# New cost figures for a list scheduler: engine handoffs, activation table loads and DMAs in a linear-attention plus SwiGLU kernel

## The chip, the cores and the metric

The program runs on one core of a Trainium2 chip. The metric is device time in microseconds (us) per execution; medians are over several executions, and all executions told here are fast, with the granted TensorE clock above 0.99 of full speed. PE is TensorE (the matmul engine), DVE is VectorE, ACT is ScalarE, POOL is GpSimd, SP is the engine whose queue issues the DMAs.

## The reference

Batch 1, 2048 tokens, width 1024, inner width 3584, 32 heads; inputs in bfloat16.

```python
x = A_x
xn = layernorm(x)
q, k, v = heads(xn @ A_wqkv)
pq, pk = phi(q), phi(k)                       # phi(t) = (t + 1 if t > 0 else exp(t)) + 1e-6
kv = einsum("bhsd,bhse->bhde", pk, v)
z  = sum over s of pk
num, den = pq @ kv, (pq . z) + 1e-6
s = (num / den) @ A_wo
g = silu((silu(xn @ B_w_gate) * (xn @ B_w_up)) @ B_w_down)
return x + s * g
```

## The kernel before

The kernel does not write its instructions in the order in which they run. It records some thousand operations in program order, each with what it reads and writes, and with an estimate of its cost. A list scheduler, at build time, plays the recorded program through a simple model of the core and so fixes one static order for each engine. A second pass adds the semaphore waits. At run time each engine works through its own list in that order. **The model's figures thus cost nothing at run time; they decide only which instruction stands before which.**

These are the parts that the change touches:

```python
LAT = {"pe": 0.25, "act": 0.3, "dve": 0.3, "pool": 0.3}      # from an engine's end to its consumer
# ... Plan.schedule(), inner loop: for each engine e that has candidates a, at its free time t
if e == "pe":
    # only the next WINDOW (6) unscheduled PE operations in program order are candidates
    rdy = [o for o in cand if o.ready <= t + 0.05]
    o = min(rdy, key=lambda o: o.idx) if rdy else min(cand, key=lambda o: (o.ready, o.idx))
else:
    rdy = [o for o in a if o.ready <= t]
    o = min(rdy, key=lambda o: (o.dl - o.boost, o.idx)) if rdy else min(a, key=lambda o: (o.ready, o.dl))
s = max(t, o.ready)
# ... the engine whose operation can start first is taken
if o.sem is not None:                      # a DMA
    free[e] = s + 0.08
    b = max(s + 1.0, dma_free)
    dma_free = b + o.nbytes / 230e3
    o.done = dma_free + 1.8
else:
    free[e] = s + o.busy
    o.done = s + o.busy + o.lat
# ...
for q in o.succs:
    q.ready = max(q.ready, o.done)
# ... cost of an activation, of a DMA issue
act: nel(o) / 1200.0 + (0.055 if src == "ps" else 0.095)
dma: 0.08
```

Start-up, in program order (cut). `ln_tile` is the layer norm of 128 tokens, `t_tile` its transposes, `p_piece(tile, 0 for K or 1 for V, half)` eight matmuls in two groups of four; `combos` are DVE sums of weight blocks:

```python
ln_tile(0); t_tile(0); ln_tile(1)
p_piece(0, 0, 1)
p_piece(0, 0, 0)
t_tile(1)
p_piece(1, 0, 1)
# ... loads of tiles 4 and 5, p_piece(1, 0, 0), ln_tile(2), p_piece(0, 1, 1), t_tile(2), combos(KVV[0]) ...
```

Of the kernel before, what the change touches and what calls it, by code (L numbers as in the profile page):

```python
# [9 lines left out]
ACT = mybir.ActivationFunctionType  # L10
# [5 lines left out]
GRAN = 256  # L16


class Op:
    __slots__ = ("eng", "fn", "busy", "lat", "nbytes", "sem", "preds", "succs", "idx", "dl", "start", "done",  # L20
                 "ev", "pecum", "npred", "ready", "urgent", "boost")


class Region:
# [6 lines left out]
class Plan:  # L31
# [1 line left out]


    ENGS = ("pe", "act", "dve", "pool", "sp")
    LAT = {"pe": 0.25, "act": 0.3, "dve": 0.3, "pool": 0.3}

    def __init__(self, window, lead):
        self.ops = []
# [6 lines left out]
    def op(self, eng, reads, writes, fn, busy, sem=None, nbytes=0, urgent=0.0, cow=None, after=None):  # L46


        o = Op()
        o.eng, o.fn, o.busy, o.sem, o.nbytes, o.urgent = eng, fn, busy, sem, nbytes, urgent  # L50
        o.lat = 0.0 if sem is not None else self.LAT[eng]
        o.boost = 0.0
        o.idx = len(self.ops)
        preds = set()
        for r in reads:
            for k in r.keys:
                preds.update(self.lastw.get(k, ()))
        if cow is not None:
            preds.update(cow.preds)
        if after is not None:  # L60
            preds.add(after)
        for r in writes:
            for k in r.keys:
                if cow is None:
                    preds.update(self.lastw.get(k, ()))
                    preds.update(self.readers.get(k, ()))
        for r in reads:
            for k in r.keys:
                self.readers.setdefault(k, []).append(o)
        for r in writes:  # L70
            for k in r.keys:
                if cow is None:
                    self.lastw[k] = [o]
                    self.readers[k] = []
                else:
                    self.lastw[k].append(o)
        o.preds = preds
        o.succs = []
        for p in preds:
            p.succs.append(o)  # L80
        o.pecum = self.pecum
        if eng == "pe":
            self.pecum += busy
            self.lastpe = o
        self.ops.append(o)
        return o

    def schedule(self):
        ops = self.ops
        for o in reversed(ops):  # L90
            d = o.pecum if o.eng == "pe" else o.pecum + 30.0
            for s in o.succs:
                extra = (4.0 + o.nbytes / 200e3) if o.sem is not None else o.busy + o.lat
                d = min(d, s.dl - extra)
            o.dl = d - o.urgent
        pes = [o for o in ops if o.eng == "pe"]
        cum = [o.pecum + o.busy for o in pes]
        for o in ops:
            if o.sem is not None and o.succs:
                k = bisect_right(cum, o.dl - self.lead) - 1  # L100
                if k >= 0 and pes[k] not in o.preds:
                    o.preds.add(pes[k])
                    pes[k].succs.append(o)
        for o in ops:
            o.npred = len(o.preds)
            o.ready = 0.0
        free = {e: 0.0 for e in self.ENGS}
        dma_free = 0.0
        avail = {e: [] for e in self.ENGS}
        pe_next = deque(o for o in ops if o.eng == "pe")  # L110
        for o in ops:
            if o.npred == 0:
                avail[o.eng].append(o)
        order = []
        done = set()
        total = len(ops)
        while len(order) < total:
            best = None
            for e in self.ENGS:
                a = avail[e]  # L120
                if not a:
                    continue
                t = free[e]
                if e == "pe":
                    lim = None
                    n = 0
                    for o in pe_next:
                        if n >= self.window:
                            lim = o.idx
                            break  # L130
                        n += 1
                    cand = [o for o in a if lim is None or o.idx < lim]
                    if not cand:
                        continue
# [3 lines that stand above are left out]
                    rdy = [o for o in a if o.ready <= t]  # L138
                    o = min(rdy, key=lambda o: (o.dl - o.boost, o.idx)) if rdy else min(a, key=lambda o: (o.ready, o.dl))
                s = max(t, o.ready)  # L140
                if best is None or s < best[0]:
                    best = (s, e, o)
            s, e, o = best
            o.start = s
            if o.sem is not None:
                free[e] = s + 0.08
                b = max(s + 1.0, dma_free)
                dma_free = b + o.nbytes / 230e3
                o.done = dma_free + 1.8
            else:  # L150
                free[e] = s + o.busy
                o.done = s + o.busy + o.lat
            avail[e].remove(o)
            if e == "pe":
                done.add(o)
                while pe_next and pe_next[0] in done:
                    pe_next.popleft()
            order.append(o)
            for q in o.succs:
                q.npred -= 1  # L160
                q.ready = max(q.ready, o.done)
                if q.npred == 0:
                    avail[q.eng].append(q)
        self.order = order
        return order
# [55 lines left out]
def build_kernel(nc, A_x, A_wqkv, A_wo, B_w_gate, B_w_up, B_w_down, out, WINDOW=6, NWARM=14, NPE=4, LEAD=12.0):  # L221
# [12 lines left out]
    with ExitStack() as es:  # L234
# [99 lines left out]
        def nel(ap):  # L334
            n = 1
            for s in ap.shape[1:]:
                n *= s
            return n

        def act(reads, writes, o, i, func, src="ps", **kw):  # L340
            return PL.op("act", reads, writes, lambda h: h.activation(o, i, func, **kw),  # L341
                         nel(o) / 1200.0 + (0.055 if src == "ps" else 0.095))

        def dve(reads, writes, fn, n, rate=0.96):
            return PL.op("dve", reads, writes, fn, n / (rate * 1000.0) + 0.07)
# [2 lines left out]
            return dve(reads, writes, lambda h: h.tensor_tensor(o, a, b, op), nel(o), 1.92 if fast else 0.96)  # L348

        def dma(reads, writes, o, i, s, nbytes, cow=None, after=None):  # L350
            return PL.op("sp", reads, writes, lambda h: h.dma_start(o, i), 0.08, sem=s, nbytes=nbytes, cow=cow,
                         after=after)

        class Ring:
# [320 lines left out]
        def t_tile(i):  # L675
            s = xnslot[i]
            xa = s.ap(FP16)
            ar, j, m = xt_dest(i)
            dst = ar.at(j * 8 * KB, 8 * KB, FP16).rearrange("p (k t) -> p k t", t=512)[:, :, m * 128:(m + 1) * 128]
            if i >= NPE:  # L680
                PL.op("sp", [s.r], [xt_r(i)], lambda h: h.dma_start_transpose(dst, xa), 0.08, sem=dsem("tx%d" % (i % 2)),
                      nbytes=400 * KB)
                return
            if not tb:
                tb.extend((balloc_part(), balloc_part()))
            for q, halves in enumerate(((0, 4), (4, 4)) if i == 0 else ((0, 8),)):
                k0, n = halves
                b = tb[(i + q) % 2]
                pb = ps[b][:, 0:n * 64].bitcast(FP16).rearrange("p (k t) -> p k t", t=128)
                pe_tr([s.r, ident_r], [bank_r[b]],  # L690
                      [(pb[:, k, :], xa[:, (k0 + k) * 128:(k0 + k + 1) * 128], ident[:, :]) for k in range(n)])
                xr = xt_r(i, k0, n)
                if q == 0 or i == 0:
                    act([bank_r[b]], [xr], dst[:, k0:k0 + n], pb, ACT.Identity)
                else:
                    dve([bank_r[b]], [xr], lambda h, k0=k0, n=n, pb=pb: h.tensor_copy(dst[:, k0:k0 + n], pb), n * 128)
# [524 lines left out]
        def d_set(p, c, Sx, sv):  # L1221
# [7 lines left out]
            def fin(i, j):  # L1229
# [18 lines left out]
                def turn_dma():  # L1248
                    o = pt_ring.take()
                    oa = o.ap(FP16).rearrange("p (m n) -> p m n", n=128)  # L1250
                    PL.op("sp", [g.r], [o.r], lambda h: h.dma_start_transpose(oa, g.ap(FP16)), 0.08,
                          sem=dsem("tp%d%d" % (link, o.k)), nbytes=200 * KB, urgent=60.0 * last)
                    tt([o.r, q.r], [q.r], xv[:, :, i * 128:i * 128 + 128], oa, xv[:, :, i * 128:i * 128 + 128], ALU.add,
                       True)
                    done()
# [196 lines left out]
```

## Time and profile before

| | before |
|---|---|
| median of the runs made beside the changed kernel | 731.93 us (731.23 to 732.62, 4 runs) |
| profiled execution | 729.5 us |
| PE, DVE, ACT busy | 98%, 84%, 55% |
| table loads on ACT | 10, of 1.28 us each |

From the page of the kernel before: busy time of each engine (share of the span, number of instructions), and the chain that ended last, by engine.

```profile
PE 715.9 (98%) x3942; PEld 371.1 (51%) x3942; DVE 612.8 (84%) x1443; ACT 400.5 (55%) x759; POOL 14.1 (2%) x35
...
PE 85%; ACT 7%; DVE 5%; issue 2%; POOL 0%; ACTq 0%; DVEq 0%; POOLq 0%
```

PE looks full. But a busy share is a poor measure for this engine: the Trainium skill says so (Perfetto Trace Analysis, Identifying the Most-Contended Engine). Two lines of the timeline of PE in the kernel before, in the steady part (start, length of the merged run, engine, line, what, count):

```profile
40.03 1.03 PE L210 MATMUL ps<-H,W 128*128 128x512 f16 x4
40.90 1.03 PE L210 MATMUL ps<-H,X 128*128 128x512 f16 x4
```

The second four matmuls start 0.87 us after the first four, so 0.216 us each; that agrees with the skill's figure of N / 2.4 + 2.5 ns for one isolated matmul of N columns (TensorE: Matmul & The Clock Gate, Back-to-back issue gap), and that page's 131 ns for sustained 512-column matmuls is not what this trace shows. A record of such a matmul lasts 0.379 us in the table of groups, though. Neighbours overlap by 0.163 us, so a wait of up to 0.163 us between two matmuls leaves "busy" unbroken.

I therefore use a second measure throughout, the **excess**: for each pair of neighbouring matmul records, the distance between their starts less (columns / 2.4 + 2.5) ns, summed over a stretch. 48 pairs of small denominator matmuls run side by side and give -5.08 us; they are left out. Where one matmul record is missing, the distance is exactly one pitch too long; that is counted as zero. In the kernel before the excess is 16.22 us of 729.5: 6.48 us in the first 120 us (about 2.7 of them slow warm-up matmuls on zeros). The rest of the run is matmuls at full pitch, 1.43 us before the first one and 5.03 us from the start of the last one to the end. So a new order can gain at most some 13.5 us, or 1.9% (an estimate: the excess less that of the warm-up). Every excess comes from one traced execution of its kernel.

Who PE waited for in the kernel before (total us, times, longest us):

```profile
PE ps L210 <- ACT TM L341: 1.7, 2, 1.3
PE ps L210 <- POOL ident L391: 1.4, 1, 1.4
PE ps L210 <- DVE ps L348: 1.4, 5, 0.4
PE ps L217 <- DVE TM L348: 1.1, 1, 1.1
PE ps L210 <- ACT X L341: 0.8, 2, 0.5
PE ps L210 <- ACT ps L341: 0.8, 3, 0.3
PE ps L217 <- ACT W L341: 0.4, 1, 0.4
PE ps L210 <- ACT H L341: 0.2, 1, 0.2
```

No DMA is in it. PE at start-up (start, length of the merged run, engine, line, what, count; in brackets: idle time just before, and what ended it):

```profile
8.27 1.04 PE L210 MATMUL ps<-H,X 128*128 128x512 bf16 x4 [0.47 <-ACT X L341]
9.15 0.61 PE L217 MATMUL ps<-ident,W 128*128 128x128 f16 x8
9.59 9.96 PE L210 MATMUL ps<-H,X 128*128 128x512 bf16 x44
...
20.25 4.49 PE L210 MATMUL ps<-H,X 128*128 128x512 bf16 x20 [0.24 <-ACT H L341]
25.19 0.62 PE L217 MATMUL ps<-ident,W 128*128 128x128 f16 x8 [0.45 <-ACT W L341]
...
27.70 1.04 PE L210 MATMUL ps<-H,X 128*128 128x512 bf16 x4 [0.38 <-ACT X L341]
...
31.78 1.90 PE L210 MATMUL ps<-H,W 128*128 128x512 f16 x8 [0.25 <-DVE ps L348]
```

DVE at start-up, 23.7 to 28.0 us. The first line, `nmean`, is the last step of DVE for the layer norm of a tile. Further on, five halves of layer-norm statistics of later tiles (24.91 to 27.41; three are cut) stand before the sums `W<-X` at 28.02. PE uses these from 28.57 on.

```profile
23.70 0.16 DVE L666 SCALAR_TENSOR_TENSOR nmean<-mv,rstd 128x1 f32<-128x1 f32 x1 [0.44 <-POOL rstd L658]
...
24.91 0.69 DVE L649 BATCH_NORM_STATS2 stats<-W 128x6 f32<-128x512 bf16 x1
...
27.41 0.68 DVE L649 BATCH_NORM_STATS2 stats<-W 128x6 f32<-128x512 bf16 x1
28.02 0.41 DVE L348 TENSOR_TENSOR W<-X 128x512 f16<-128x512 f16 x1
```

And a table load on ACT with what surrounds it. PE issues one matmul at 136.66 and then nothing until 138.31, waiting for the activation that had to wait for the load:

```profile
136.37 1.28 ACT L341 ACT_TABLE_LOAD   x1
...
136.66 0.38 PE L210 MATMUL ps<-H 128*128 128x512 bf16 x1
...
137.66 0.60 ACT L341 ACTIVATE TM<-ps 128x512 f16<-128x512 f32 x1
...
138.31 0.88 PE L210 MATMUL ps<-H 128*128 128x512 bf16 x3 [1.27 <-ACT TM L341]
```

The previous activation ends at 136.35 and the next starts at 137.66, so a switch of tables costs 1.3 us here between the records, nearly all of it the load. By the distance of starts, which is 1.93 us across the switch and 0.48 us between the two activations before it, it costs some 1.45 us.

### The profile page before, as it was taken

Reading aid. Unit: us, or ns where it says so; the run is one execution under the profiler, and the core shown is the slowest. Engines: PE = TensorE matmul, PEld = TensorE weight load, DVE = VectorE, ACT = ScalarE, POOL = GpSimd, SP = SyncE. Lnnn points to the kernel's source line nnn. Section 1 sums busy time; section 2 is a strip of 40 time slices with the busy share of each in tenths; the row PEclk is TensorE's granted clock in tenths of the full one; section 3 lists DMA queues with packets and bytes.
Section 4 is the critical chain, followed back from the end, with each engine's and each line's share of the span. In section 5 each row is a group of like instructions: output and inputs, shape, how many; then the busy total and the mean of one; then the engine's idle time right before and its main releaser. Section 6 shows DMA issues by size and latency. Waiting matters only on the chain.

```text
span 729.5 us, 10728 instructions
## 1 busy us (share of the span) xinstructions
PE 715.9 (98%) x3942; PEld 371.1 (51%) x3942; DVE 612.8 (84%) x1443; ACT 400.5 (55%) x759; POOL 14.1 (2%) x35
## 2 busy tenths in 40 slices
PE   8999999999999999999999999999999999999996
PEld 3444444455555555554444445555555555544442
DVE  6999868979989998898555989999999888865662
ACT  3776654787659665654111177676966756511111
POOL 2111000000000000000000000000000000000000
PEclk9999999999999999999999999999999999999999
DMA  8443235135255343324279554134515343546633
GB/s 291 113 104 85 44 107 181 59 107 168 73 159 139 129 143 129 94 73 132 79 186 245 145 165 149 62 116 120 172 59 188 102 130 118 143 123 181 164 89 87
DMA packets 135668, 94.02 MB, mean 129 GB/s; under 512 B 32960, under 2 KB 131520, under 8 KB 135616
## 3 DMA queue, kind: packets, MB, share of 16 engines
q1 hardware_dynamic: 135616, 93.34, 44.9%
q8 instruction: 31, 0.51, 0.3%
q14 instruction: 21, 0.17, 0.1%
HBM read 75.50 MB, written 10.62 MB: 118 GB/s over the span
## 4 chain that ended last, share of the span: by engine, by line
PE 85%; ACT 7%; DVE 5%; issue 2%; POOL 0%; ACTq 0%; DVEq 0%; POOLq 0%
PE ps L210 85%; ACT H L341 3%; ACT TM L341 2%; DVE W L348 2%; DVE H L348 1%; DVE TM L348 1%; ACT ps L341 1%; DVE ps L348 1%; ACT L341 1%; DVE stats L649 0%; DVE stats L653 0%; DVE TM L724 0%; PE ps L217 0%; DVE X L348 0%; POOL rstd L658 0%
## 5 line engine op out<-in xcount | busy, mean ns | idle before, releaser
L210 PE MATMUL ps<-X,W 128*128 128x512 f16 (+1 forms) x1232 | 268.0, 358 | 1.1 <-ACT ps L341 0.5
L341 ACT ACTIVATE TM<-ps 128x512 f16<-128x512 f32 (+2 forms) x345 | 184.2, 553 | 147.8 <-PE ps L210 143.9
L210 PE MATMUL ps<-H,W 128*128 128x512 f16 (+2 forms) x1168 | 256.4, 369 | 0.5 <-DVE ps L348 0.5
L348 DVE TENSOR_TENSOR W<-W 128x256 f16<-128x256 f16 (+5 forms) x440 | 176.4, 437 | 7.2 <-DMA W<-in_B_w_down_dram 7.0
L210 PEld LDWEIGHTS ps<-H,W 128*128 128x128 f16 (+1 forms) x1168 | 113.5, 98 | 124.1 <-DVE ps L348 2.3
L210 PEld LDWEIGHTS ps<-X,W 128*128 128x128 f16 (+1 forms) x1232 | 119.3, 98 | 102.8 <-ACT ps L341 2.2
L348 DVE TENSOR_TENSOR ps<-ps,TM 128x256 f32<-128x256 f32 (+1 forms) x234 | 123.5, 531 | 15.0 <-PE ps L210 14.0
L341 ACT ACTIVATE ps<-ps 128x512 f32<-128x512 f32 (+1 forms) x164 | 81.9, 499 | 72.2 <-PE ps L210 70.1
L210 PE MATMUL ps<-P,W 128*128 128x512 f16 (+1 forms) x496 | 104.7, 329 | 0.7 <-ACT TM L341 0.4
L341 ACT ACTIVATE H<-ps 128x512 f16<-128x512 f32 (+1 forms) x126 | 75.0, 602 | 54.5 <-PE ps L210 54.2
L210 PEld LDWEIGHTS ps<-P,W 128*128 128x128 f16 (+1 forms) x496 | 48.3, 98 | 37.9 <-ACT ps L341 1.0
L348 DVE TENSOR_TENSOR H<-H 128x1024 f16<-128x1024 f16 (+4 forms) x106 | 66.1, 640 | 1.0 <-ACT H L341 0.5
L348 DVE TENSOR_TENSOR TM<-ps,TM 128x512 f32<-128x512 f32 (+1 forms) x60 | 40.7, 678 | 24.0 <-PE ps L210 23.7
L210 PE MATMUL ps<-W 128*128 128x256 f16 (+1 forms) x278 | 56.5, 289 | 0.6 <-DVE ps L348 0.4
L348 DVE TENSOR_TENSOR H<-H,TM 128x512 f16<-128x512 f16 x112 | 44.8, 415 | 14.0 <-ACT H L341 13.8
L341 ACT ACTIVATE TM<-TM 128x512 f16<-128x512 f32 (+1 forms) x61 | 37.9, 624 | 33.4 <-DVE TM L348 32.5
L210 PEld LDWEIGHTS ps<-W 128*128 128x128 f16 (+1 forms) x278 | 26.1, 98 | 21.3 <-DVE ps L348 2.3
L210 PE MATMUL ps<-H,X 128*128 128x512 bf16 (+1 forms) x136 | 32.2, 379 | 1.2 <-ACT X L341 0.8
L210 PE MATMUL ps<-TM,W 128*128 128x256 f16 (+1 forms) x138 | 27.8, 283 | 0.3 <-DVE ps L348 0.3
L348 DVE TENSOR_TENSOR P<-H 128x1024 f16<-128x1024 f16 x28 | 19.0, 686 | 9.2 <-PE ps L210 9.2
L723 DVE TENSOR_SCALAR TM<-TM 128x512 f16<-128x512 f16 x64 | 17.7, 285 | 10.5 <-ACT TM L341 10.3
L348 DVE TENSOR_TENSOR H<-ps,TM 128x512 f16<-128x512 f32 (+1 forms) x35 | 23.9, 682 | 2.3 <-PE ps L210 1.7
(81 smaller groups left out, 394.9 us busy)
## 6 DMA issues: line engine op xcount, KB each, us to landing
W<-in_B_w_down_dram SPq DMA_DIRECT2D x16, 896.0 KB, 5.8
W<-in_B_w_gate_dram SPq DMA_DIRECT2D x12, 1024.0 KB, 5.4
W<-in_B_w_up_dram SPq DMA_DIRECT2D x12, 1024.0 KB, 5.5
W<-in_A_x_dram SPq DMA_DIRECT2D x16, 256.0 KB, 3.0
H<-in_A_wqkv_dram SPq DMA_DIRECT2D x8, 512.0 KB, 8.2
H<-r_scratch SPq DMA_DIRECT2D x32, 128.0 KB, 3.4
W<-m_scratch SPq DMA_DIRECT2D x4, 1024.0 KB, 5.9
s_scratch<-TM SPq DMA_DIRECT2D x32, 128.0 KB, 2.8
```

Source lines behind the costliest of these rows:

```text
L210: last = h.matmul(o, l, r, start=st, stop=sp, skip_group_check=True)
L341: return PL.op("act", reads, writes, lambda h: h.activation(o, i, func, **kw), nel(o) / 1200.0 + (0.055 if src == "ps" else 0.095))
L348: return dve(reads, writes, lambda h: h.tensor_tensor(o, a, b, op), nel(o), 1.92 if fast else 0.96)
L723: dve([e.r], [b.r], lambda h: h.tensor_scalar(ba, ea, 1.0, EPS_PHI, ALU.min, ALU.add), 512, 2.6)
```

## The change

The intent: give the planner figures read from a trace. Handoffs between engines get shorter, one PE operation may follow another on PE without a handoff, a table load costs 1.28 us of ACT, activations with a bias or a scale operand get slower, a DMA takes 0.47 us (a transposing one 1.22 us) of SP to issue, starts to move 1.8 us after its issue instead of 1.0, moves 340 GB/s instead of 230 (loads of 128 and 896 KB are planned as 1.45 times as large), and is planned to be usable 2.0 us after its last byte instead of 1.8.

```diff
+TABLE, DMA_SLACK = 1.28, 2.0
-    LAT = {"pe": 0.25, "act": 0.3, "dve": 0.3, "pool": 0.3}
+    LAT = {"pe": 0.2, "act": 0.165, "dve": 0.14, "pool": 0.15}
@@ schedule
                 s = max(t, o.ready)
+                if e == "act" and o.tab is not None and o.tab != tab:
+                    s += TABLE
@@
             s, e, o = best
+            if o.tab is not None:
+                tab = o.tab
             if o.sem is not None:
-                free[e] = s + 0.08
-                b = max(s + 1.0, dma_free)
-                dma_free = b + o.nbytes / 230e3
-                o.done = dma_free + 1.8
+                free[e] = s + o.busy
+                b = max(s + 1.8, dma_free)
+                dma_free = b + o.nbytes / 340e3
+                o.done = dma_free + DMA_SLACK
@@
-                q.ready = max(q.ready, o.done)
+                q.ready = max(q.ready, o.done if q.eng != "pe" or o.eng != "pe" else s + o.busy)
@@ act
-                         nel(o) / 1200.0 + (0.055 if src == "ps" else 0.095))
+                      nel(o) / (1000.0 if "bias" in kw or not isinstance(kw.get("scale", 1.0), float) else 1200.0)
+                      + (0.055 if src == "ps" else 0.095))
+            q.tab = func if func != ACT.Identity else None
@@ dma, and the two transposing DMAs
-            ... h.dma_start(o, i), 0.08, sem=s, nbytes=nbytes, ...
+            ... h.dma_start(o, i), 0.47, sem=s, nbytes=nbytes * (1.45 if nbytes in (128 * KB, 896 * KB) else 1.0), ...
-            ... h.dma_start_transpose(...), 0.08, ...
+            ... h.dma_start_transpose(...), 1.22, ...
```

(Cut: the new slot `tab` and its first value.)

More of the change, by code (lines that the diff above doesn't have):

```diff
@@ L16 @@
 GRAN = 256
+TABLE, DMA_SLACK = 1.28, 2.0
 class Op:
     __slots__ = ("eng", "fn", "busy", "lat", "nbytes", "sem", "preds", "succs", "idx", "dl", "start", "done",
-                 "ev", "pecum", "npred", "ready", "urgent", "boost")
+                 "ev", "pecum", "npred", "ready", "urgent", "boost", "tab")
 class Region:
@@ L52, in op @@
         o.boost = 0.0
+        o.tab = None
         o.idx = len(self.ops)
@@ L108, in schedule @@
         dma_free = 0.0
+        tab = None
         avail = {e: [] for e in self.ENGS}
@@ L340, in act @@
         def act(reads, writes, o, i, func, src="ps", **kw):
-            return PL.op("act", reads, writes, lambda h: h.activation(o, i, func, **kw),
-                         nel(o) / 1200.0 + (0.055 if src == "ps" else 0.095))
+            q = PL.op("act", reads, writes, lambda h: h.activation(o, i, func, **kw),
+                      nel(o) / (1000.0 if "bias" in kw or not isinstance(kw.get("scale", 1.0), float) else 1200.0)
+                      + (0.055 if src == "ps" else 0.095))
+            q.tab = func if func != ACT.Identity else None
+            return q
         def dve(reads, writes, fn, n, rate=0.96):
@@ L350, in dma @@
         def dma(reads, writes, o, i, s, nbytes, cow=None, after=None):
-            return PL.op("sp", reads, writes, lambda h: h.dma_start(o, i), 0.08, sem=s, nbytes=nbytes, cow=cow,
+            return PL.op("sp", reads, writes, lambda h: h.dma_start(o, i), 0.47, sem=s,
+                         nbytes=nbytes * (1.45 if nbytes in (128 * KB, 896 * KB) else 1.0), cow=cow,
                          after=after)
@@ L680, in t_tile @@
             if i >= NPE:
-                PL.op("sp", [s.r], [xt_r(i)], lambda h: h.dma_start_transpose(dst, xa), 0.08, sem=dsem("tx%d" % (i % 2)),
+                PL.op("sp", [s.r], [xt_r(i)], lambda h: h.dma_start_transpose(dst, xa), 1.22, sem=dsem("tx%d" % (i % 2)),
                       nbytes=400 * KB)
@@ L1250, in turn_dma @@
                     oa = o.ap(FP16).rearrange("p (m n) -> p m n", n=128)
-                    PL.op("sp", [g.r], [o.r], lambda h: h.dma_start_transpose(oa, g.ap(FP16)), 0.08,
+                    PL.op("sp", [g.r], [o.r], lambda h: h.dma_start_transpose(oa, g.ap(FP16)), 1.22,
                           sem=dsem("tp%d%d" % (link, o.k)), nbytes=200 * KB, urgent=60.0 * last)
```

## The prediction

> **What bounds the kernel now.** TensorE. The page gives PE 715.9 of 729.5 us busy (98%), DVE 84%, ACT 55%, DMA 45%, full clock. The Trainium skill (Perfetto Trace Analysis, Identifying the Most-Contended Engine) warns that matmul busy share is no measure of headroom, so I added up start-to-start distances of the matmul records. Consecutive 128x512 matmuls start 0.216 us apart when nothing is awaited; at that rate the columns explain about 707 us. What is left: 1.4 us before the first matmul, 2.5 us of slow warm-up matmuls, 4.8 us after the last matmul (final add, output DMA), and about 11 us of waits between matmuls. By the timeline these sit at 8-32 us (3.2 us; start-up: layer norm, weight sums, transposes on DVE and ACT), 134-140 (2.4, ACT, at a table load), 230-245 (1.5, an ACT burst of scalings by zc), 417-437 (1.6, DVE full, three table loads of 1.28 us in 6 us), 467 (0.4), 518-530 (1.0), 724 (1.3). Elsewhere there are almost none. The list of PE's waits shows no DMA.
>
> **What the change does.** No arithmetic is removed or added: matmuls, ten table loads, DVE/ACT operations and DMAs stay. Only each engine's static order moves. The planner's costs come closer to the trace: ACT start to matmul 0.78 -> 0.65 us for 128x512 (trace 138.63 -> 139.29: 0.66); DVE 0.90 -> 0.74 (trace 31.03 -> 31.78: 0.75); a DMA issue 0.08 -> 0.47 us (trace 0.47), a transposing one 1.22 (trace 1.20-1.35); 230 -> 340 GB/s (trace 340 in 10-20 us); table load 0 -> 1.28 us (trace and the skill's ScalarE: Activation LUTs, What ACT_TABLE_LOAD costs, agree; the further drain that page adds shows as no gap here). A matmul group no longer waits in the plan for the group before it, so TensorE's order is less chopped: 776 rows of like instructions in the built program instead of 889.
>
> **How much is on the critical path.** Only the roughly 10 us of waits. Longer runs into one bank are no faster: 0.216 us either way. Start-up looks mixed: the new order runs all 16 first K matmuls before tile 1's transposes. With the old landings (10.14 and 11.65 us for the last two weight blocks) TensorE would wait about 0.75 us for weights and 1 us for the ACT copy of the transposes; part comes back because DVE no longer takes statistics for tiles 5 and 6 ahead of sums that TensorE awaits (25-30 us). At the tail the last DVE add and first output DMA change places: up to 0.4 us worse. At 134-140, 230-245 and 417-437 us I expect a third to a half of 5.5 us back. Net gain 1 to 4 us.
>
> **Predicted time.** 729.6 us (before 731.87), 80% range 726.0 to 733.0. Faster by over 2%: 0.02; within 2%: 0.96; slower by over 2%: 0.02.
>
> **What would show it.** Right: waits of PE from 8 down to 6-8 us in total; first 32 us up to 1 us longer; less wait around 134-140 and 417-437; tail equal within 0.5 us; ten table loads. Wrong: start-up changes by over 2 us, or DMA waits appear in PE's list.
>
> **What would make it wrong.** Margins cut from 0.3 to 0.14-0.165 us leave TensorE many small waits in stretches that have none now (160-300, 440-600 us, DVE 95% full): +3 us. Or the less chopped order gives DVE/ACT results later and moves whole waits. Or almost all waits go: 724 us.

## The result, and the profile after

| | before | after |
|---|---|---|
| median, 4 runs each, same rounds | 731.93 us | 728.98 us (728.57 to 729.46) |
| ratio, 95% interval | | 0.9960 (0.9943 to 0.9977) |
| profiled execution | 729.5 us | 727.4 us |
| excess of PE, whole run | 16.22 us | 13.90 us |
| start of the last matmul to the end | 5.03 us | 5.24 us |

A ratio is the mean time of one kernel's fast runs over that of the other's fast runs of the same rounds, so it is not quite the ratio of the medians quoted. The two traced executions differ by 2.1 us: 2.3 us less excess, 0.2 us more tail.

The same two lines of the page of the changed kernel. (Line numbers moved by 9 to 13; 14 matmul records are missing, so PE busy is no measure of the gain.)

```profile
PE 712.1 (98%) x3928; PEld 372.0 (51%) x3942; DVE 612.7 (84%) x1443; ACT 400.2 (55%) x759; POOL 14.4 (2%) x35
...
PE 92%; DVE 4%; ACT 1%; DMA 1%; issue 0%; SPq 0%; DVEq 0%
```

Who PE waited for in the changed kernel:

```profile
PE ps L219 <- ACT TM L350: 1.8, 3, 1.0
PE ps L219 <- ACT X L350: 1.6, 2, 1.2
PE ps L219 <- POOL ident L404: 1.4, 1, 1.4
PE ps L226 <- DVE TM L360: 1.1, 1, 1.1
PE ps L219 <- DMA H<-in_A_wqkv_dram: 1.0, 3, 0.5
PE ps L219 <- DVE ps L360: 0.9, 2, 0.5
PE ps L219 <- ACT ps L350: 0.9, 1, 0.9
PE ps L226 <- DVE W L676: 0.4, 1, 0.4
PE ps L219 <- DVE W L360: 0.2, 1, 0.2
```

The list adds up to 9.3 us, against 7.8 us before, although PE waited less: the list counts only the part of a wait that outlasts the previous record. DMA is in the list now, three waits in start-up. PE at start-up:

```profile
7.98 1.04 PE L219 MATMUL ps<-H,X 128*128 128x512 bf16 x4 [0.47 <-ACT X L350]
9.18 1.02 PE L219 MATMUL ps<-H,X 128*128 128x512 bf16 x4 [0.16 <-DMA H<-in_A_wqkv_dram]
10.60 1.04 PE L219 MATMUL ps<-H,X 128*128 128x512 bf16 x4 [0.39 <-DMA H<-in_A_wqkv_dram]
12.09 1.04 PE L219 MATMUL ps<-H,X 128*128 128x512 bf16 x4 [0.46 <-DMA H<-in_A_wqkv_dram]
12.96 0.61 PE L226 MATMUL ps<-ident,W 128*128 128x128 f16 x8
14.73 5.35 PE L219 MATMUL ps<-H,X 128*128 128x512 bf16 x23 [1.16 <-ACT X L350]
...
23.82 0.61 PE L226 MATMUL ps<-ident,W 128*128 128x128 f16 x8
```

The 16 first K matmuls of tile 0 now run before the transposes of tile 1 (12.96), three times waiting for weights, and the next matmuls at 14.73 wait for the ACT copy of those transposes. After that start-up runs almost without stops. DVE's order differs in two ways. Its last step for tile 3 (`nmean`) comes at 21.55 instead of 23.70, and PE transposes that tile at 23.82 without a stop, instead of at 25.19 after one. And `W<-X` stands at 26.39, with statistics of later tiles behind it, at 30.28 and later; since no stop of PE before is put down to `W<-X`, this second difference is not shown to have gained anything.

```profile
21.55 0.15 DVE L679 SCALAR_TENSOR_TENSOR nmean<-mv,rstd 128x1 f32<-128x1 f32 x1
...
24.67 0.68 DVE L666 BATCH_NORM_STATS2 stats<-W 128x6 f32<-128x512 bf16 x1
25.27 1.20 DVE L360 TENSOR_TENSOR H<-H 128x2048 f16<-128x2048 bf16 x1
26.39 0.41 DVE L360 TENSOR_TENSOR W<-X 128x512 f16<-128x512 f16 x1
...
30.28 0.68 DVE L662 BATCH_NORM_STATS2 stats<-W 128x6 f32<-128x512 bf16 x1
```

The first of the later table loads, as before. PE waits from after 135.63 to 137.00:

```profile
135.05 1.28 ACT L350 ACT_TABLE_LOAD   x1
...
135.63 0.38 PE L219 MATMUL ps<-H 128*128 128x512 bf16 x1
...
136.34 0.60 ACT L350 ACTIVATE TM<-ps 128x512 f16<-128x512 f32 x1
...
137.00 0.60 PE L219 MATMUL ps<-H 128*128 128x512 bf16 x2 [0.99 <-ACT TM L350]
```

Excess of PE by stretch (us, worked out as above, from the two traces):

| stretch, us | before | after | |
|---|---|---|---|
| 0-34 | 6.12 | 6.00 | start-up |
| 34-120 | 0.36 | 0.23 | |
| 120-215 | 2.83 | 1.43 | table loads at 136, 163, 176 us |
| 215-395 | 1.82 | 1.89 | |
| 395-515 | 2.49 | 1.19 | table loads at 424, 428, 430, 441, 464, 476 us |
| 515 to the end | 2.61 | 3.16 | |

So the gain lies in the stretches where the table loads are, 2.7 us of it; start-up only changed its form, and 515 us to the end lost 0.55 us. It lies in these stretches, but little of it in the stops for the loads themselves. At the first one the stop for the load shrank by 0.29 us of excess (1.44 at 138.31, 1.15 at 137.00 after). Three other stops near it went away: 0.47 us for DVE at 134.44 and 0.26 for ACT at 134.93, before the load, and 0.28 for ACT at 139.29. In 395-515 us most of the stops of the kernel before, too, were for results of DVE.

### The profile page after: what moved, and what is told of

Its sections match the earlier page's. It is cut to its first block, busy times and chain, and to the rows that moved or that the text cites. A ratio compares the mean times of both kernels' runs of the same rounds, so it can differ in the third digit from the quotient of the medians.

```text
span 727.4 us, 10731 instructions
## 1 busy us (share of the span) xinstructions
PE 712.1 (98%) x3928; PEld 372.0 (51%) x3942; DVE 612.7 (84%) x1443; ACT 400.2 (55%) x759; POOL 14.4 (2%) x35
## 4 chain that ended last, share of the span: by engine, by line
PE 92%; DVE 4%; ACT 1%; DMA 1%; issue 0%; SPq 0%; DVEq 0%
PE ps L219 92%; DVE H L360 2%; DMA H<-in_A_wqkv_dram 1%; DVE W L360 1%; DVE ps L360 1%; ACT TM L350 1%; ACT L350 0%; SPq L363 0%; DVE TM L360 0%; PE ps L226 0%; ACT ps L350 0%; ACT X L350 0%; DVE H L737 0%; ACT H L350 0%; DVEq L243 0%
## 5 line engine op out<-in xcount | busy, mean ns | idle before, releaser
L219 PE MATMUL ps<-H,W 128*128 128x512 f16 (+2 forms) x1162 | 250.4, 369 | 0.3
L219 PE MATMUL ps<-P,W 128*128 128x512 f16 (+1 forms) x496 | 100.1, 329 | 0.6 <-ACT TM L350 0.6
L219 PE MATMUL ps<-H,P 128*128 128x512 bf16 (+1 forms) x94 | 23.1, 379 | 0.1
L219 PEld LDWEIGHTS ps<-H,X 128*128 128x128 f16 x136 | 12.7, 98 | 18.3 <-ACT X L350 2.0
```

What stands on the lines that cost most here:

```text
L219: last = h.matmul(o, l, r, start=st, stop=sp, skip_group_check=True)
```

## The experiments

The change has three parts, named by letters: **H**, handoffs (the four latencies and the PE-to-PE rule); **T**, table loads and slower activations; **D**, DMA figures. Twelve kernels were run, each with five timed rounds beside the kernel before; all gave correct results. The arithmetic is the same in all of them, only the order differs.

### One part alone (first four runs)

`only_lat`, H's first half:

```diff
-    LAT = {"pe": 0.25, "act": 0.3, "dve": 0.3, "pool": 0.3}
+    LAT = {"pe": 0.2, "act": 0.165, "dve": 0.14, "pool": 0.15}
```

> The kernel before with only the four engine latencies changed (0.25/0.3/0.3/0.3 to 0.2/0.165/0.14/0.15 us). Theory A, accurate handoffs: every wait of TensorE in the kernel before was on ACT, DVE or GpSimd, so this part carries most of the gain of 2.95 us: 729.0 to 730.0 us, and the waits at 134-140 and 417-437 us shrink as in the changed kernel. Theory B, reshuffle: any new constant only draws another order; this part alone lands anywhere from 729 to 734 us, and the four parts do not add up to the whole (sum of their gains off from 2.95 by over 2 us).

Measured: 735.45 us against 731.41, ratio 1.0056 (1.0043 to 1.0069). Slower by 4 us: theory A fell with its first run. The time is also beyond theory B's range of 729 to 734. The excess rose from 16.22 to 20.26 us, in most stretches.

`only_pepe`, H's second half:

```diff
-                q.ready = max(q.ready, o.done)
+                q.ready = max(q.ready, o.done if q.eng != "pe" or o.eng != "pe" else s + o.busy)
```

> The kernel before with only the rule that a matmul group is ready for the next group of TensorE at its issue end, without latency. This part makes most of the change in TensorE's order (719 lines differ from before, 292 from the changed kernel). Theory A: longer runs are no faster, the pitch stays 0.216 us, and results for ACT and DVE come earlier for some groups and later for others: within 1 us of before, 731.0 to 732.5. Theory B: anywhere from 729 to 734, and the start-up loss of the changed kernel (a stop of 1.3 us before the matmul at 14.7 us) appears here already, since it comes from the order of the first K pieces.

Measured: 736.35 us, ratio 1.0067 (1.0055 to 1.0080). Neither form of theory A; for theory B the time is even beyond the range. The start-up stop that it named did not appear in that form (0.9 us before, 1.4 us here, at 8 to 20 us).

`only_table`, T alone (cut: the slot `tab` and the line that keeps it):

```diff
+                if e == "act" and o.tab is not None and o.tab != tab:
+                    s += TABLE
-                         nel(o) / 1200.0 + ...
+                      nel(o) / (1000.0 if "bias" in kw or ... else 1200.0) + ...
```

> The kernel before with only the table load (1.28 us) and the slower activations with a bias or a scale operand in the plan. Theory A: ten loads, of which four lie near waits of TensorE: gain 0 to 0.8 us, 731.1 to 731.9, with less wait at 134-140 and 423-430 us. Theory B: anywhere from 729 to 734, with changed waits in stretches that have no table load.

Measured: 731.03 us against 731.41, ratio 0.9994 (0.9980 to 1.0007): no change that stands clear of the noise, and just below theory A's range. But inside it two things cancel: around the table loads the excess fell from 5.32 to 3.54 us, in the first 120 us it rose from 6.48 to 8.55 us, a stretch without later table loads, as theory B had it.

`only_dma`, D alone (cut: the issue costs of 0.47 and 1.22 us and the factor 1.45, as in the whole change):

```diff
-                free[e] = s + 0.08
-                b = max(s + 1.0, dma_free)
-                dma_free = b + o.nbytes / 230e3
-                o.done = dma_free + 1.8
+                free[e] = s + o.busy
+                b = max(s + 1.8, dma_free)
+                dma_free = b + o.nbytes / 340e3
+                o.done = dma_free + 2.0
```

> The kernel before with only the DMA figures (issue 0.47 and 1.22 us, 340 GB/s, start 1.8 us, margin 2.0 us, larger 128 and 896 KB loads). Theory A: TensorE waited for no DMA before, so 731.2 to 732.6, no gain; start-up may show DMA waits of up to 1 us, as the plan now expects the weights earlier. Theory B: anywhere from 729 to 734. Theory C, the gain is mostly DMA: 729.5 or less, with transposing DMAs issued earlier in 30-120 us or fewer waits of DVE for DMA.

Measured: 733.01 us, ratio 1.0028 (1.0015 to 1.0040). Slower, by 1.6 us in the medians and 2.0 by the ratio, which includes one execution of 735.40 us among five; just above theory A's range, and theory C fell as far as D alone goes.

If the effects of the four single edits added up, their sum, +10 us, would be expected for the whole change, which gained 3. So the parts depend on each other, and a new theory was needed.

### Two parts of the three (next runs)

`only_handoff` has both halves of H. The other three are the changed kernel with one part put back: `no_table` is H and D, `no_dma` is H and T, `no_handoff` is T and D. Their edits are those above, put together or undone. `no_handoff` was run last, together with the kernels of the next section; theory A2, which its expectation names, was formed after the other three.

```diff
# only_handoff, on the kernel before
+    LAT = {"pe": 0.2, "act": 0.165, "dve": 0.14, "pool": 0.15}
+                q.ready = max(q.ready, o.done if q.eng != "pe" or o.eng != "pe" else s + o.busy)
# no_table, on the changed kernel
-                    s += TABLE
-                      nel(o) / (1000.0 if "bias" in kw or ... else 1200.0) + ...
# no_dma, on the changed kernel
+                dma_free = b + o.nbytes / 230e3        # and 0.08, 1.0, 1.8 as before, no factor 1.45
# no_handoff, on the changed kernel
+    LAT = {"pe": 0.25, "act": 0.3, "dve": 0.3, "pool": 0.3}
+                q.ready = max(q.ready, o.done)
```

> Latencies and the TensorE-to-TensorE rule together, on the kernel before; each alone was slower (735.45 and 736.35 us). Theory D, the two belong together: a plan that has only one of them runs TensorE at a pace that differs from its consumers', and with both the gain appears: 731.0 us or less. Theory B, reshuffle: parts scatter by several us whatever their accuracy; this lands anywhere from 730 to 738, and is as likely as not above 734.

Measured: 733.90 us against 731.26, ratio 1.0033 (1.0020 to 1.0046). The two halves partly repair each other (1.0056 and 1.0067 alone), but no gain appears: theory D, that the halves of H belong together and pay then, fell; theory B's wide range holds the time.

> The changed kernel without the table loads (and without the slower activations) in its plan. Theory D with small table effect: only_table alone gained 0.4 us, so 729.0 to 730.0. Theory B: anywhere from 728 to 735.

Measured: 731.88 us, ratio 1.0007 (0.9994 to 1.0019). Table loads are not a small effect once H and D are there: without them the whole gain is gone.

> The changed kernel without its DMA figures. Theory D with DMA irrelevant or harmful (alone it cost 1.6 us, in start-up): 728.0 to 729.5, and the start-up loss at 8-20 us (2.85 us in the changed kernel, 0.94 before) falls below 1.5 us. Theory C, the DMA figures are what pays: 731.5 us or more. Theory B: anywhere from 728 to 737.

Measured: 732.05 us, ratio 1.0007 (0.9993 to 1.0020). The DMA figures, harmful alone, are needed for the gain too, as theory C said; theory D's sign, less than 1.5 us at 8-20 us, failed as well (2.44 us). Start-up shows one place. PE in the run without D:

```profile
22.20 4.49 PE L219 MATMUL ps<-H,X 128*128 128x512 bf16 x20 [0.78 <-ACT H L350]
...
28.68 1.04 PE L219 MATMUL ps<-H,X 128*128 128x512 bf16 x4 [0.76 <-ACT X L350]
...
33.31 2.76 PE L219 MATMUL ps<-H,W 128*128 128x512 f16 x12 [1.00 <-DVE ps L360]
```

These stops of 0.8 to 1.0 us at 22 to 33 us are missing in the changed kernel. In the trace of this run DVE again has statistics of two later tiles (26.53 to 28.43 us) ahead of the sums at 28.98 us, as in the kernel before, but the stop at 28.68 is for ACT. What comes late for it is tile 3: its `nmean` stands at 25.30 us here and at 21.55 in the changed kernel. In the four plans with D this step comes at 21.4 to 23.0 us, in the four without at 23.7 to 25.3 us. All four plans without D have 2.1 to 3.4 us of excess at 20-34 us; the four with D have 0.02 to 0.94 us there (but more at 8-20 us).

> The changed kernel with the old engine latencies and the old TensorE-to-TensorE rule, so table loads and DMA figures alone. With the seven other combinations this completes the three parts taken with and without each other. If the parts added up it would be 731.4 - 0.4 + 1.6 = 732.6 us. Theory A2, a plan is only as good as its worst figure, so that the gain shows only with all three: 731.5 to 733.5. Theory B: 729 to 735.

Measured: 730.65 us against 731.35, ratio 0.9990 (0.9978 to 1.0003). Below theory A2's range, and better than the sum of the parts.

The eight combinations, with the time against the kernel before (ratio less one, times 731.4 us) and the excess of PE in three kinds of stretches:

| parts | time against before, us | excess 0-120 us | around table loads (120-215, 395-515) | elsewhere |
|---|---|---|---|---|
| none (before) | 0 | 6.48 | 5.32 | 4.43 |
| H | +2.4 | 6.85 | 7.53 | 4.08 |
| D | +2.0 | 7.20 | 5.82 | 4.13 |
| H, D | +0.5 | 7.38 | 4.87 | 4.57 |
| T | -0.4 | 8.55 | 3.54 | 4.18 |
| T, H | +0.5 | 8.73 | 3.32 | 4.77 |
| T, D | -0.7 | 8.00 | 2.86 | 3.92 |
| T, H, D (after) | -2.9 | 6.23 | 2.61 | 5.05 |

Each time has an interval of about 1 us to both sides. Three things can be read off:

- **T acts where the tables are loaded, in every company**: adding it lowers the third column by 1.8 (to nothing), 4.2 (to H), 3.0 (to D) and 2.3 us (to H and D). Over all fourteen traces the eight plans with T have 2.3 to 3.5 us there and the six without have 4.9 to 7.7, so this is no lucky draw. Which half of T does it, the table loads or the slower activations, was not tested.
- **T costs start-up, unless H and D are both there**: the second column rises by 2.1, 1.9 and 0.8 us in the first three cases, and falls by 1.2 us in the last. This is weaker: the four variants of the changed kernel tested below have 5.8 to 7.3 us in that column, so that differences of about 1 us there can be the draw of one order.
- H and D do not pay by themselves. The last one added gains most: T 3.4, D 3.4, H 2.2 us.

So the net gain over the kernel before, 2.3 us of excess, is 2.7 us around the table loads, of which T alone brings 1.8, then 0.25 us at start-up, and a loss of 0.6 us elsewhere. Against T alone, H and D bring 2.3 us at start-up and 0.9 around the loads, and cost 0.9 elsewhere. Why they do so is not shown.

### Is it accuracy, or a lucky draw?

`lat_more` and `lat_less` are the changed kernel with latencies off by about a tenth:

```diff
-    LAT = {"pe": 0.2, "act": 0.165, "dve": 0.14, "pool": 0.15}
+    LAT = {"pe": 0.22, "act": 0.18, "dve": 0.155, "pool": 0.165}     # lat_more
+    LAT = {"pe": 0.18, "act": 0.15, "dve": 0.125, "pool": 0.135}     # lat_less
```

> The changed kernel with its four engine latencies 8 to 11% larger (0.22, 0.18, 0.155, 0.165 us): figures that are off by at most 0.02 us, a tenth of what the change corrected. Theory A2, accuracy pays and the parts need each other: within 0.7 us of the changed kernel, 728.3 to 729.7. Theory B, reshuffle: each plan is a draw from orders that scatter with a spread of about 2 us around 732, and the changed kernel is a good draw: 729.5 to 735, at least 0.8 us above the changed kernel.

> The changed kernel with its four engine latencies 10% smaller (0.18, 0.15, 0.125, 0.135 us). Theory A2: 728.3 to 730.0, perhaps with more waits under 0.2 us. Theory B: 729.5 to 735, at least 0.8 us above the changed kernel in one or both of this and the run with larger latencies.

Measured: 729.39 and 729.33 us, ratio 0.9972 (0.9960 to 0.9985) for both; the changed kernel had 0.9960. Both times lie inside theory A2's ranges and just below theory B's. But by the ratios, which compare each kernel with the kernel before in its own rounds, both are 0.9 us above the changed kernel: more than the 0.7 that theory A2 allowed, and more than the 0.8 that theory B asked for. So these two runs do not decide between the theories. The excess around the table loads is 2.31 and 2.92 us, near the changed kernel's 2.61. About two thirds of the gain survives; some 0.9 us of it may be luck, which the intervals do not settle. Nor is either a wholly new draw: matched by operation and operands, over 90% of DVE's instructions in the two traces stand in the order of the changed kernel, against about 65% in the kernel before.

`slack_half` changes the margin of the DMAs:

```diff
-TABLE, DMA_SLACK = 1.28, 2.0
+TABLE, DMA_SLACK = 1.28, 0.5
```

> The changed kernel with a DMA margin of 0.5 us instead of 2.0. Theory S, the margin pays: landings vary, a plan without margin stops engines for late data, 730.5 to 733, with DMA among the waits of TensorE or DVE growing by over 1 us. Theory A2 without the margin, TensorE waits for DMA only in the first 13 us, where the plan's start is set by the first landing: 728 to 730. Theory B: anywhere from 729 to 735, with the loss in stretches that have no DMA wait.

Measured: 728.15 us against 731.35, ratio 0.9954 (0.9940 to 0.9967). Theory S fell by the time: a quarter of the margin does as well, and the DMA waits of PE stay three, of 1.0 us in all. Its sign did appear, on DVE: the waits of DVE for DMA grew from 20.3 to 28.8 us in the list of waits, and the time did not rise. This is also the widest redraw of the four variants, with DVE's order no nearer to the changed kernel (about 65%) than the kernel before is, and it keeps the gain. It is the fastest kernel, but its interval overlaps that of the changed kernel. Start-up excess rose to 7.26 us, the other stretches gave it back (2.28 around the loads, 3.92 elsewhere), and the tail was 4.62 us.

### The start-up stop

`tile1_first` takes away the 1.16 us stop at 14.73 us in the changed kernel by moving one call:

```diff
         p_piece(0, 0, 1)
+        t_tile(1)
         p_piece(0, 0, 0)
-        t_tile(1)
```

> The changed kernel with one call moved: the transposes of tile 1 stand before the second half of tile 0's K pieces. Theory E, the 1.3 us stop before the matmul at 14.7 us is an accident of order that costs its full length: waits at 8-20 us fall from 2.85 to about 1 us, those at 20-34 stay near 0, 726.5 to 727.5 us. Theory F, start-up is paced by the DVE and ACT work, as in the kernel before: the wait reappears at 20-34 us (0.04 becomes 1.5 to 2.5 us), and the time stays at 728.5 to 729.5.

Measured: 728.55 us against 731.26, ratio 0.9962 (0.9949 to 0.9974), the same as the changed kernel. Theory E fell. PE in this run:

```profile
8.36 1.93 PE L219 MATMUL ps<-H,X 128*128 128x512 bf16 x8 [0.47 <-ACT X L350]
10.90 0.62 PE L226 MATMUL ps<-ident,W 128*128 128x128 f16 x8 [0.61 <-DVE W L676]
...
19.48 3.63 PE L219 MATMUL ps<-H,X 128*128 128x512 bf16 x16 [0.30 <-DVE TM L737]
```

The stop for the ACT copy is gone, and PE stops for DVE instead: 0.61 us for the normalised tile 1 (L676) at 10.90, and 0.30 us at 19.48. In DVE's order a sum of weight blocks stands ahead of that normalisation; DVE idles 1.63 us for the weights to land, works on the sum from 9.15 to 10.38, and only then normalises tile 1. Theory F is right in kind, with one correction: the wait came back mostly within the first 20 us (2.23 us at 8-20 us against 2.85), not at 20-34 us (0.32 against 0.04). Over 0-34 us the excess went from 6.00 to 5.41 us; a gain of 0.6 us is below what the timing resolves.

## Why the prediction was right or wrong

**The time was right**: 729.6 us forecast, 728.98 measured, inside the range; a gain of 1 to 4 us forecast, 2.95 measured. The bound was right: only order changed, the pitch of 0.216 us did not, and the waits between matmuls were all there was to gain. But the 80% range, 726.0 to 733.0, also holds no change at all, and nothing in the forecast says why all of the figures together should gain when H and D together, T and H together, or T alone show no gain clear of the noise. That the middle of the range was hit is in part luck.

**"At 134-140, 230-245 and 417-437 us I expect a third to a half of 5.5 us back": right in the sum, not in each.** With the stretches widened to hold the shift of both kernels, the excess went from 2.57 to 1.26 us at 120-145 us and from 1.70 to 0.75 us at 395-445 us, but from 1.74 to 1.87 us at 215-250 us. Together 2.1 of 6.0 us came back, all of it in the stretches with table loads, though mostly not in the stops for the loads themselves. The ACT burst by zc at 230 us has no table load in it and kept its waits; its counterpart at 515-540 us even grew from 1.13 to 1.77 us.

**"Start-up looks mixed": right in the balance, not in the reason for what comes back.** About 0.75 us of waiting for weights and 1 us for the ACT copy were forecast; the list of waits shows 1.0 us and 1.16 us, the excess 1.50 and 1.32. DVE did take the statistics of later tiles after the sums, as forecast, and 0-34 us came out equal (6.12 and 6.00 us). But no stop of TensorE in the kernel before is put down to those sums. What the traces show in its place is that DVE finishes tile 3 earlier (21.55 instead of 23.70 us), and the stops at 20-34 us, for results of ACT and DVE, fall from 2.42 to 0.04 us. "Up to 1 us longer" did not happen.

**"Waits of PE from 8 down to 6-8 us in total": wrong as stated.** The list of waits rose from 7.8 to 9.3 us while the excess fell from 16.22 to 13.90 us. The step that failed is the choice of the measure: each listed wait is short by the 0.163 us by which the previous record sticks out, and waits shorter than that are not listed at all. The kernel before has 19 waits of 0.06 to 0.2 us, the changed one 8.

**"DMA waits appear in PE's list" as a sign of error contradicted the text itself**, which forecast 0.75 us of waiting for weights. They appeared as forecast, and the step did not fall.

**Tail: "up to 0.4 us worse"**: 5.03 to 5.24 us. Right. Ten table loads stayed ten.

**What the forecast did not see** is that the parts fight each other. It judged the change as a whole and said nothing of what its parts do to each other. In the runs, shorter latencies alone cost 4.0 us, the PE-to-PE rule alone 4.9, the DMA figures alone 1.6 (by the medians). The feared "many small waits in stretches that have none now" are real in the run with the latencies alone but not in the full change: in the two stretches named, 160-300 and 440-600 us, the excess is 4.1 us before, 8.4 with the latencies alone and 4.3 after.

Open: why a plan with some right and some wrong figures is worse than one with all wrong. That wrong figures offset each other (a long latency standing in for an unmodelled table load, for instance) would fit, but no run shows it directly. Also open is which half of T costs start-up; its slower activations with a bias run there (layer norm), its later table loads do not, and the halves were not run apart. And no close variants of the kernel before, or of the plans with one or two parts, were run, so how much of each of their times is the luck of one order is not known.

## What to carry to other kernels

In a planned kernel, change the cost figures together and judge them together: one figure made right can cost more than it brings while its neighbours are still wrong, and the sum of single tests (+10 us here) says nothing about the whole (-3 us). Judge by stretches of the run, not by the total: T, the table figure with the slower activations, looked worthless alone, because 1.8 us gained in the stretches with the loads were lost at start-up. And measure TensorE's waits by the distance of matmul starts, since the records overlap and both the busy share and the list of waits hide short stops.

## What the Trainium skill lacked or had wrong

- TensorE: Matmul & The Clock Gate, Back-to-back issue gap, gives about 131 ns per matmul as the sustained figure for 512 columns in a stream with weight loads. Here it is 216 ns in the steady stretches (four matmuls in 0.866 us, each with its own weight load), which is that page's formula for the isolated gap.
- Perfetto Trace Analysis, Identifying the Most-Contended Engine, warns of matmul busy share but does not say that waits between matmuls are hidden: records of 379 ns at a pitch of 216 ns hide 163 ns of each stop, so that listed waits rose by 1.5 us while the real ones fell by 2.3 us.
- ScalarE: Activation LUTs, What ACT_TABLE_LOAD costs, adds a drain of about 1380 ns to the 1283 ns load for every switch. At the switch at 136.37 us ACT is idle or loading for 1.3 us between two activations (some 1.45 us lost by the distance of starts), so no such drain shows.
- DMA: Bandwidth & Descriptors gives the issue cost of a transposing DMA only as cycle counts in its table of a later chip's improvements, and no time measured on this one. In the kernel before, 35 of 43 take 1.19 to 1.35 us of SP (the others up to 4.08), and 201 of 214 plain ones take 0.30 to 0.60 us.
